# Top-k attention: eight candidates of the smaller halves instead of sixteen, a guarded second computation, and a mask by ReLU and GpSimd

## The chip, the cores and the metric

The kernel runs on one core of a Trainium2 chip. The metric is device time in microseconds of one execution, lower is better. The core has five engines that run side by side and meet only at semaphores: TensorE (PE in the profile, with its weight loads as PEld), VectorE (DVE), ScalarE (ACT), GpSimd (POOL) and SyncE (SP), which here issues nearly all transfers. Each engine takes its instructions strictly in the order in which the program lists them.

## The reference, cut to what matters

The inputs are q, k and v of shape (8, 8, 576, 64) (batch, heads, sequence, head width), a gain of 512 and two weight matrices of 512 x 2048 and 2048 x 512.

```python
# attention, per batch and head
scores = scale * q @ k.T                          # 576 x 576, scale = 1/8
kth = 32nd largest score of each row
scores = where(scores >= kth, scores, -1e9)
attn = exp(scores - row_max); attn /= attn.sum + 1e-9
x = attn @ v                                      # heads side by side: (8, 576, 512)
# feed-forward
xn = (x - mean) / sqrt(var + 1e-6) * g_ln
out = x + relu(xn @ w_ch1) @ w_ch2
```

All is fp32. There are 8 x 8 x 576 = 36,864 rows of 576 scores, and the 32nd largest of each has to be found.

## The kernel before, in words

**Units.** The attention is cut into 160 units. A full unit (128 of them) is 128 query rows of two heads of one batch: two tiles `t` of 128 x 576 scores. A rest unit (32) holds the last 64 rows of the sequence for two heads, as one tile of 128 x 576. A job is a batch and a pair of heads (`hp`) with its groups of units; units of a group share one transposed probability tile `pt`.

**One unit, step by step.** `scores` (L412 matmuls, L393 copies by ACT) writes the scores to `sc`. `halve` (L433 and on) splits each row into two halves of 288 and keeps, for each pair of columns, the larger in `hi` and the smaller in `lo`: the larger by a DVE maximum (L433), the smaller by two exact integer passes on POOL (a - hi, L438, and + b, L441); only the first unit takes a DVE minimum (L436). `select` then finds the 32 largest. DVE's MAX8 gives the eight largest of a row, and a match-replace (a load of the eight values, then a pass) overwrites them with -3e38. First two MAX8 over `lo` (L453), with a replace between (L448), put the 16 largest of the smaller halves into the last 16 columns of `hi`, which is therefore 304 wide; then four rounds of MAX8 over `hi` (L462), with replaces between the rounds (L448), give the 32 largest, eight at a time. The first eight hold the row's maximum (`u.top`), the last of the fourth eight is the threshold (`u.thr`). `prepare` makes the exponential's bias from both (L478 on DVE for the first units, L483 and L484 on POOL later). `mask` (L489) is one ACT operation, a leaky ReLU of (threshold - score) with slope 2^-90, so that scores at or over the threshold keep a scaled value and the others stay large; `weigh` (L499) is the exponential, with the row sums as its second output. The probabilities are transposed, either by PE (`turn`: L553, L573, L574, L582, with ACT copies into `pt`) or, for units marked `moved`, by DVE in blocks and through DRAM (`move`: L531, two DMAs L536 and L539). `values` (L607, L614) multiplies by v, `place` (L626, L649) normalises into rows of x.

**Feed-forward.** When two row tiles of x are complete they form a `Block` (18 in all): statistics on DVE (L677, L678), centring on POOL (L686), transposes (L711), hidden products (L752, ReLU on ACT L775), projections (L909, in seven products instead of eight, with POOL sums L839 to L845 and joins L889, L893), scaling (L730) and the residual (L723). The first block projects plainly (L791). Weights arrive in pieces that ACT, POOL and DVE convert (L190 to L208) until about unit 17 (`CONVERTING`).

**Order.** The order is written out by hand: the program disables the scheduler, and the order of issue in the source is the order on each engine. The main loop has one step `n` per unit. Step n selects unit n, masks unit n - 1 (`mk`), weighs and transposes unit n - 2 (`ex`), and computes the scores of unit n + 2; in the first units (`EARLY`, the first eight) mask and weigh of unit n - 1 stand together near the step's start. Between these pieces `fill()` inserts feed-forward matmuls from the list `todo`. How many is decided by a planner: during the conversion of weights from the difference of assumed DVE and PE costs of a step (`dve_cost`, with DVE_UNIT = 8.6 and DVE_REST = 5.0), later by spreading evenly what is left up to the next block. Buffers that matter here: `sc` five, `hi` two, `lo` one, `e` (masked scores and probabilities) two, five PSUM banks for scores and transposes and three for products.

## Time and profile before

| | |
|---|---|
| Time, median of 3 runs | 1653.51 us (1651.67 to 1654.98) |
| Profiled execution, own time | 1652.03 us |
| Its span, first to last instruction | 1650.0 us |
| Mean granted TensorE clock | 0.959 |
| Selection over `hi`: MAX8 L462 | x1152, mean 462 ns |
| Selection over `hi`: replace L448 | x864, mean 460 ns |
| Selection over `lo`: MAX8 L453 | x576, mean 443 ns |
| Selection over `lo`: replace L448 | x288, mean 443 ns |
| Larger halves, DVE L433 | x160, mean 692 ns |
| Smaller halves, POOL L438 and L441 | x159 each, mean 1286 and 1285 ns |
| Mask and exponential, ACT L489 and L499 | x288 each, mean 782 and 783 ns |

A line of the profile names the source line, the engine, the operation, output and input with shapes, the count, then the engine's busy time in us and the mean of one in ns; behind the last bar stands the time in which the engine was idle just before these instructions, and what ended it. A window row gives the stretch in us, its length, busy time and count for each engine, then the granted TensorE clock, the share of the DMA engines and GB/s. A timeline row gives start, length, engine, line and operation. Durations of neighbouring instructions on one engine can overlap.

### The profile page before, as it was taken

The page shows a single profiled execution, that of the slowest core. Times are in us where ns is not written, and L with a number is a line of the kernel's source. Part 1 is how long each engine was busy: PE and PEld are TensorE (multiplying, and loading weights), DVE is VectorE, ACT ScalarE, POOL GpSimd, SP SyncE. Part 2 cuts the span into 40 slices and gives each one's busy share as a digit, 9 for nine tenths or more (in the row PEclk, how much of TensorE's full clock was granted, in tenths as well). Part 3 has the DMA queues.
Part 4 walks back from the last instruction along what each step waited for, and adds up shares of the span by engine and source line. Part 5 has one row for each costly group of instructions (what it writes and reads, how often), then busy time and mean ns, then how long its engine had stood idle before and what let it go on. Part 6 is the DMA issues. An engine that isn't in the chain of part 4 may idle for free.

```text
span 1650.0 us, 27871 instructions
## 1 busy us (share of the span) xinstructions
PE 1504.6 (91%) x7897; PEld 1134.6 (69%) x7897; DVE 1458.2 (88%) x4652; ACT 1064.0 (64%) x2712; POOL 958.4 (58%) x1492
## 2 busy tenths in 40 slices
PE   3569998999888988999999998999989999999998
PEld 1336566767655766777677776777767777778887
DVE  5999898999999999999999999999999999994000
ACT  6987876767655756667566665676657766654411
POOL 4778759555555564656564656474646564655243
PEclk6679999999999999999999999999999999999999
DMA  7533355113454455535555456535564455532211
GB/s 200 131 128 114 100 119 143 55 58 90 124 156 136 124 144 160 159 94 139 171 165 162 114 128 177 168 105 135 153 184 134 130 131 169 154 114 83 73 51 51
DMA packets 358945, 211.46 MB, mean 128 GB/s; under 512 B 250756, under 2 KB 331144, under 8 KB 358792
## 3 DMA queue, kind: packets, MB, share of 16 engines
q1 hardware_dynamic: 354056, 209.10, 44.9%
q10 hardware_dynamic: 4736, 0.59, 0.3%
q8 instruction: 63, 1.03, 0.3%
q14 instruction: 90, 0.74, 0.2%
HBM read 145.62 MB, written 63.96 MB: 127 GB/s over the span
## 4 chain that ended last, share of the span: by engine, by line
DVE 65%; PE 19%; POOL 7%; ACT 3%; DMA 2%; issue 2%; SPq 1%; DVEq 0%; POOLq 0%; ACTq 0%
DVE m L462 19%; DVE hi L448 17%; DVE hi L453 10%; PE hps L752 8%; PE ops L909 6%; DVE lo L448 6%; DVE hi L433 5%; DVE sc L531 4%; PE av L607 2%; PE scps L412 1%; POOL lo L441 1%; POOL lo L438 1%; DVE st L677 1%; DVE kT L342 1%; POOL w L208 1%
## 5 line engine op out<-in xcount | busy, mean ns | idle before, releaser
L752 PE MATMUL hps<-xT,w 128*128 128x256 f32 x2304 | 547.5, 383 | 1.9 <-ACT xT L714 1.9
L462 DVE MAX8 m<-hi 128x8 f32<-128x304 f32 x1152 | 489.5, 462 | 3.3
L752 PEld LDWEIGHTS hps<-xT,w 128*128 128x128 f32 x2304 | 422.0, 191 | 71.6 <-issue 15.4
L438 POOL TENSOR_TENSOR lo<-sc,hi 128x576 int32<-128x576 int32 (+1 forms) x159 | 204.5, 1286 | 451.3 <-DVE hi L433 224.3
L448 DVE MATCH_REPLACE8 hi<-m,hi 128x304 f32<-128x304 f32 x864 | 391.1, 460 | 0.0
L909 PE MATMUL ops<-w,h 128*128 128x256 f32 x1360 | 325.6, 383 | 1.7 <-POOL h L845 1.7
L909 PEld LDWEIGHTS ops<-w,h 128*128 128x128 f32 x1360 | 248.6, 191 | 42.9 <-issue 6.9
L453 DVE MAX8 hi<-lo 128x8 f32<-128x288 f32 x576 | 234.2, 443 | 7.5 <-POOL lo L441 6.4
L393 ACT COPY sc<-scps 128x288 f32<-128x288 f32 x576 | 195.8, 409 | 58.2 <-PE scps L412 21.0
L499 ACT ACTIVATE e<-e,bias 128x576 f32<-128x576 f32 x288 | 225.5, 783 | 9.6 <-POOL bias L484 9.0
L489 ACT ACTIVATE e<-sc,m 128x576 f32<-128x576 f32 x288 | 225.0, 782 | 5.8 <-DVE m L462 3.2
L441 POOL TENSOR_TENSOR lo<-lo,sc 128x576 int32<-128x576 int32 (+1 forms) x159 | 204.3, 1285 | 12.5
L607 PE MATMUL av<-pt,vb 128*64 128x256 f32 (+2 forms) x1088 | 158.1, 435 | 47.2 <-DMA pt<-turned 24.5
L607 PEld LDWEIGHTS av<-pt,vb 128*64 128x64 f32 x1088 | 81.6, 149 | 115.4 <-issue 42.2
L775 ACT ACTIVATE h<-hps 128x512 f32<-128x512 f32 x144 | 86.1, 598 | 115.8 <-PE hps L752 115.3
L412 PE MATMUL scps<-kT,late_qT 64*128 64x288 f32 (+3 forms) x832 | 128.7, 411 | 7.9 <-ACT pt L565 5.3
L909 PE MATMUL ops<-wt,s 128*128 128x256 f32 x544 | 129.2, 381 | 0.0
L448 DVE MATCH_REPLACE8 lo<-hi,lo 128x288 f32<-128x288 f32 x288 | 125.6, 443 | 0.0
L531 DVE STREAM_TRANSPOSE sc<-e 128x512 f32<-128x512 f32 x144 | 93.8, 685 | 35.0 <-ACT e L499 34.9
L433 DVE TENSOR_TENSOR hi<-sc 128x576 f32<-128x576 f32 (+1 forms) x160 | 110.8, 692 | 10.0 <-ACT sc L393 10.0
L553 PE MATMUL tp<-ident,e 128*128 128x128 f32 x576 | 91.7, 284 | 29.9 <-ACT e L499 28.3
L412 PE MATMUL scps<-kT,qT 64*128 64x288 f32 x512 | 92.3, 461 | 27.9 <-DVE qT L342 26.1
(96 smaller groups left out, 1843.9 us busy)
## 6 DMA issues: line engine op xcount, KB each, us to landing
turned<-sc SPq DMA_DIRECT2D x72, 512.0 KB, 2.6
pt<-turned SPq DMA_DIRECT2D x288, 128.0 KB, 2.9
w<-forms SPq DMA_DIRECT2D x136, 256.0 KB, 3.8
vb<-in_v_dram SPq DMA_DIRECT2D x136, 128.0 KB, 3.2
raw<-in_moe_w_ch_dram SPq DMA_DIRECT2D x32, 512.0 KB, 4.2
kT<-kept SPq DMA_DIRECT2D x36, 288.0 KB, 3.3
kin<-in_k_dram SPq DMA_DIRECT2D x128, 72.0 KB, 2.5
kept<-kT SPq DMA_DIRECT2D x32, 288.0 KB, 3.1
```

The lines of the kernel that those rows point to most:

```text
L393: nc.scalar.copy(u.sc[:, t, s * HALF : (s + 1) * HALF], made[s][t][:, 0:HALF])
L412: nc.tensor.matmul(ps[i * R : i * R + ql, o : o + width], qT[r, q0 : q0 + ql], kT[r, k0 : k0 + width], start=True, stop=True,)
L438: nc.gpsimd.tensor_tensor(lo.bitcast(I32), a.bitcast(I32), hi.bitcast(I32), ALU.subtract)
L441: nc.gpsimd.tensor_tensor(lo.bitcast(I32), lo.bitcast(I32), b.bitcast(I32), ALU.add)
L448: nc.vector.match_replace(x[:, t], m[:, t, :], x[:, t], LOWEST)
L453: nc.vector.max(u.hi[:, t, o : o + 8], u.lo[:, t])
L462: nc.vector.max(m[:, t, :], u.hi[:, t])
L489: nc.scalar.activation(u.e[:, t], u.sc[:, t], AF.Prelu, bias=u.thr[:, t, 7:8], scale=-1.0, alpha=SLOPE)
L499: nc.scalar.activation(u.e[:, t], u.e[:, t], AF.Exp, bias=u.bias[:, t : t + 1], scale=-scale / SLOPE, accum_out=g.den[:, col : col + 1],)
L607: nc.tensor.matmul(av[h * D : (h + 1) * D, 0 : g.nq], vb[:, h * J + c, :], g.blocks[:, h, 0 : g.nq // 32, c, :], start=(c == 0), stop=False,)
L752: nc.tensor.matmul(ps[0][:, side * N : (side + 1) * N], w1[:, c, f * P : (f + 1) * P], self.xT[:, c, 0:N], start=(c == 0), stop=(c == NC - 1),
L909: nc.tensor.matmul(bank[name][:, 0:Q], a(j), rhs, start=first and j == 0, stop=(j == G - 1), skip_group_check=not first,)
```

## The change

- `select` takes only the eight largest of the smaller halves (`low_rounds=1`): one MAX8 over `lo` per tile, no replace. `hi` is 296 wide instead of 304; its first two rounds read only the 288 larger halves, and the eight candidates of `lo` are found in the second round and join in the third and fourth.
- `halve` takes the smaller halves by a DVE minimum for every unit; POOL's two integer passes are gone.
- `mask` becomes a ReLU of 2^90 x (threshold - score) on ACT, followed by a POOL subtraction of the scores; the exponential's scale and bias follow. `prepare` writes the scaled threshold (`edge`) and the bias into spare columns of the threshold's tile: two small operations, on DVE for the first units and on POOL later.
- `watch` notes, per unit, the eighth candidate of the smaller halves minus the threshold; a value of zero or more means that a ninth could have belonged to the 32. DVE reduces these notes every 16 units, and `tell` turns them into one flag at the end.
- The kernel becomes `compute(low_rounds=1)`, then a read of the flag on every engine, and behind a branch the whole `compute(low_rounds=2)` again.
- The planner's DVE_UNIT becomes 6.0 + 1.65 x low_rounds = 7.65 and DVE_REST 0.58 of it. In the first units both masks are issued before both exponentials. Two small statistics tiles come from a pool with two buffers instead of four.

```diff
         u.lo = lopool.tile([P, 2, HALF], FP32, tag="lo", name="lo")
-        u.hi = hipool.tile([P, 2, HALF + TOP_K // 2], FP32, tag="hi", name="hi")
+        u.hi = hipool.tile([P, 2, HALF + 8 * low_rounds], FP32, tag="hi", name="hi")
         a, b = u.sc[:, 0:nt, 0:HALF], u.sc[:, 0:nt, HALF:S]
         lo, hi = u.lo[:, 0:nt], u.hi[:, 0:nt, 0:HALF]
         nc.vector.tensor_tensor(hi, a, b, ALU.max)
-        if u.i == 0:
-
-            nc.vector.tensor_tensor(lo, a, b, ALU.min)
-            return
-        nc.gpsimd.tensor_tensor(
-            lo.bitcast(I32), a.bitcast(I32), hi.bitcast(I32), ALU.subtract
-        )
-        nc.gpsimd.tensor_tensor(lo.bitcast(I32), lo.bitcast(I32), b.bitcast(I32), ALU.add)
+        nc.vector.tensor_tensor(lo, a, b, ALU.min)
...
-        if i == 0:
-            for o in range(HALF, HALF + TOP_K // 2, 8):
+        if i == 1:
+            for r in range(low_rounds):
+                o = HALF + 8 * r
                 for t in nt:
                     nc.vector.max(u.hi[:, t, o : o + 8], u.lo[:, t])
-                if o == HALF:
+                if r < low_rounds - 1:
                     for t in nt:
-                        replace(u.hi[:, :, o : o + 8], t, u.lo)
-            return
-        for r in ((0,), (1,), (2, 3))[i - 1]:
-            pl = brief_small if r in (1, 2) else small
-            m = pl.tile([P, 2, 8], FP32, tag=f"m{r}", name=f"m{r}")
+                        replace(u.hi[:, :, o : o + 8], t, u.lo[:, t])
+        width = HALF + 8 * low_rounds if i > 1 else HALF
+        pl = brief_small if i in (1, 2) else small
+        m = pl.tile([P, 2, 8], FP32, tag=f"m{i}", name=f"m{i}")
+        for t in nt:
+            nc.vector.max(m[:, t, :], u.hi[:, t, 0:width])
+        if i < TOP_K // 8 - 1:
             for t in nt:
-                nc.vector.max(m[:, t, :], u.hi[:, t])
-            if r < TOP_K // 8 - 1:
-                for t in nt:
-                    replace(m, t, u.hi)
...
     def prepare(u):
...
+        u.bias, u.edge = u.thr[:, 0:nt, 5], u.thr[:, 0:nt, 6]
+        if doubt is not None:
+            watch(u)
+        eng = nc.vector if u.i < CONVERTING else nc.gpsimd
+        eng.tensor_scalar(u.edge, u.thr[:, 0:nt, 7], STEEP, 0.0, ALU.mult, ALU.add)
+        eng.tensor_scalar(u.bias, u.top[:, 0:nt, 0], -scale, 0.0, ALU.mult, ALU.add)
+
+    def watch(u):
...
+        eng.tensor_tensor(
+            watched[:, c : c + nt], u.hi[:, 0:nt, HALF + 7], u.thr[:, 0:nt, 7], ALU.subtract
+        )
+        if u.i % 16 == 15 or u.i == N - 1:
+            u.ends_watch = True
+
+    def settle_watch():
+
+        for out, first, op in ((0, 0, ALU.max), (33, 1, ALU.min)):
+            nc.vector.tensor_reduce(
+                watched[:, out : out + 1], watched[:, first : first + 33],
+                mybir.AxisListType.X, op,
+            )
+
+    def tell():
+
+        w = hpool.tile([P, J * P], FP32, tag="h", name="tell")
+        nc.gpsimd.memset(w[:], 0.0)
+        nc.vector.tensor_scalar(w[:, 1:2], watched[:, 33:34], -1.0e38, None, ALU.is_le)
+        nc.vector.tensor_scalar(w[:, 0:1], watched[:, 0:1], 0.0, None, ALU.is_ge)
+        nc.vector.tensor_tensor(w[:, 0:1], w[:, 0:1], w[:, 1:2], ALU.max)
+        ps = brief("tell")
+        nc.tensor.transpose(ps[:, 0:P], w[:, 0:P], ident[:])
+        nc.vector.tensor_reduce(w[0:1, P : P + 1], ps[0:1, 0:P], mybir.AxisListType.X, ALU.max)
+        nc.vector.tensor_copy(doubt, w[0:1, P : P + 1])
 
     def mask(u, t):
         if u.e is None:
             u.e = epool.tile([P, 2, S], FP32, tag="e", name="e")
         nc.scalar.activation(
-            u.e[:, t], u.sc[:, t], AF.Prelu, bias=u.thr[:, t, 7:8], scale=-1.0, alpha=SLOPE
+            u.e[:, t], u.sc[:, t], AF.Relu, bias=u.edge[:, t : t + 1], scale=-STEEP
         )
+        nc.gpsimd.tensor_tensor(u.e[:, t], u.e[:, t], u.sc[:, t], ALU.subtract)
...
-            u.e[:, t], u.e[:, t], AF.Exp, bias=u.bias[:, t : t + 1], scale=-scale / SLOPE,
+            u.e[:, t], u.e[:, t], AF.Exp, bias=u.bias[:, t : t + 1], scale=-scale,
...
-    DVE_UNIT, DVE_REST, DVE_MOVE, DVE_TURN = 8.6, 5.0, 1.4, 1.45
+    DVE_UNIT = 6.0 + 1.65 * low_rounds
+    DVE_REST, DVE_MOVE, DVE_TURN = 0.58 * DVE_UNIT, 1.4, 1.45
...
         if early:
             for t in range(2):
                 mask(ex, t)
+            for t in range(2):
                 weigh(ex, t)
...
+        if doubt is not None and at(n - 1) and at(n - 1).ends_watch:
+            settle_watch()
+            if n == N:
+                tell()
...
+    doubt = ctx.enter_context(tc.tile_pool(name="doubt", bufs=1)).tile(
+        [1, 1], I32, tag="doubt", name="doubt"
+    )
+    compute(tc, *operands, low_rounds=1, doubt=doubt[:])
+    again = nc.values_load(
+        doubt[:], min_val=0, max_val=1,
+        skip_runtime_bounds_check_because="a comparison's result",
+    )
+    with tc.If(again > 0):
+        compute(tc, *operands, low_rounds=2, doubt=None)
```

## The prediction

> **What bounds the kernel now.** I read the busy shares first, then the chain that ended last, then the windows by stage, because the chain changes engine on the way.
>
> ```profile
> PE 1504.6 (91%) x7897; PEld 1134.6 (69%) x7897; DVE 1458.2 (88%) x4652; ACT 1064.0 (64%) x2712; POOL 958.4 (58%) x1492
> ...
> DVE m L462 19%; DVE hi L448 17%; DVE hi L453 10%; PE hps L752 8%; PE ops L909 6%; DVE lo L448 6%; DVE hi L433 5%; DVE sc L531 4%; PE av L607 2%; PE scps L412 1%; POOL lo L441 1%; POOL lo L438 1%; DVE st L677 1%; DVE kT L342 1%; POOL w L208 1%
> ```
>
> Two engines are near full by busy time, and the chain (65% DVE, 19% PE) runs on the selection of the 32 largest. Three middle stages, with 0 to 200 before them and a last stretch after 1500 (columns: PE, weight load, DVE, ACT, POOL busy, then clock and DMA):
>
> ```profile
> 0.00:50.00 50.00, 15.17 (x53) 9.41 (x55) 31.94 (x95) 34.37 (x69) 28.25 (x34) 0.65 0.66 165
> 50.00:200.00 150.00, 117.65 (x531) 74.61 (x532) 140.51 (x472) 129.15 (x296) 115.64 (x103) 0.84 0.44 130
> ...
> 200.00:400.00 200.00, 189.93 (x1092) 136.46 (x1091) 191.19 (x618) 145.65 (x387) 131.50 (x196) 0.99 0.34 87
> 400.00:700.00 300.00, 267.39 (x1397) 198.38 (x1395) 295.05 (x933) 189.57 (x506) 160.62 (x270) 0.95 0.51 142
> 700.00:1500.00 800.00, 771.36 (x4129) 592.79 (x4128) 786.76 (x2500) 521.48 (x1359) 458.45 (x767) 0.99 0.50 142
> ```
>
> From 400 to 1500 DVE is 98% busy: it sets the pace. From 1500 on it has nothing to do; PE runs the last projections alone for 150 us. So a saving on DVE counts until PE is full, and the question is how near PE is.
>
> **PE's room: a rule against a row.** By busy time PE has 96% in 700 to 1500, so 29 us of room in 800. The Trainium skill (Trainium Kernel Development and Optimization, Performance Expectations) says that matmul busy time is a poor measure of how near TensorE is to its limit, because matmuls are pipelined, and that the weight loads are a better one. The trace lets me count instead, from spacings in the last stretch, where PE never waits:
>
> ```profile
> 1505.28 1.95 PE L607 MATMUL av<-pt,vb 128*64 128x256 f32 x16
> 1507.16 0.70 PE L614 MATMUL av<-pt,ends 128*128 128x256 f32 x2
> ...
> 1591.14 27.79 PE L752 MATMUL hps<-xT,w 128*128 128x256 f32 x128
> 1618.77 10.52 PE L909 MATMUL ops<-w,h 128*128 128x256 f32 x48
> ```
>
> Start to start that is 27.63/128 = 0.216 us for one of L752 or L909, 1.88/16 = 0.118 for L607, 0.53/2 = 0.265 for L614; likewise 0.146 for L412 (8 in 1.17), 0.11 for a transpose, and 0.432 for L791 (twice the columns of L752, an estimate). Times the counts of each line in a stage:
> - 200 to 400: 399 of L752 and L909 (86.2), 36 of L791 (15.6), 192 of L607 (22.6), 24 of L614 (6.4), 214 of L412 (31.2), 227 transposes (25): 187 us of need in 200.
> - 400 to 700: 737, 0, 192, 24, 278, 166: 247 in 300.
> - 700 to 1500: 2341, 0, 544, 68, 706, 470: 742 in 800.
>
> The need is 93%, 82% and 93%; the rule is right that busy time hides room. Mixed work has reached at most 97% (96.7 us of need between 1100 and 1200, counted the same way), so I divide by 0.97: 193, 255 and 765 us. By busy time the last stage could give at most 29 us, by the count 35, and the middle one 33 or 45.
>
> **Part 1: DVE, selection.** One full unit (two heads by 128 rows), from the timeline:
>
> ```profile
> 902.39 0.07 DVE L448 MATCH_VALUE_LOAD lo<-hi,lo 128x8 f32 x1
> 902.45 0.44 DVE L448 MATCH_REPLACE8 lo<-hi,lo 128x288 f32<-128x288 f32 x1
> ...
> 903.24 0.81 DVE L453 MAX8 hi<-lo 128x8 f32<-128x288 f32 x2
> 903.96 0.84 DVE L462 MAX8 m<-hi 128x8 f32<-128x304 f32 x2
> ...
> 905.59 0.75 DVE L433 TENSOR_TENSOR hi<-sc 128x576 f32<-128x576 f32 x1
> 906.26 0.85 DVE L462 MAX8 m<-hi 128x8 f32<-128x304 f32 x2
> ```
>
> - Removed: the pair of replaces on the smaller halves (902.39 to 903.24, 0.85 us) and the second pair of maxima (903.24 to 903.96, 0.72 us): 1.57 us. I use starts, not durations: durations overlap, and their sum would be a fifth more.
> - Narrowed: rounds 0 and 1 read 288 columns instead of 304 (8 instructions), rounds 2 and 3 read 296 (6). The rows give (0.460 - 0.443)/16 = 1.06 ns a column, so 8 x 16 + 6 x 8 = 176 columns, 0.19 us.
> - Added: the minimum of the halves, now always on DVE, two inputs, 128x576. It has one row of its own (L436, 752 ns, at 12 us); its twin L433 takes 0.67 from start to start.
>
> Net 1.57 + 0.19 - 0.67 = 1.09 us for each of 128 full units, half for each of 32 rest units: 157 us. Back go the watch's reductions (10 sets of two), the larger preparation of the first units (one more small operation, 0.2 us, in some 17) and the verdict's five small ones: about 9 us, at rows of 0.16 to 0.20. Net 148 of 1458, 9.9 us per 100.
>
> **Part 2: POOL.** It loses the two integer passes (409 us) and the bias pair (56), and gains the subtraction e - sc, 288 of 128x576 at 1.41 (the median of L438 for that size; fp32 at 128x512 takes 1.27 in L723, the same per column): 406; and three small operations for 143 units: 86. It ends near 985. The GPSIMD Engine Reference (section 1, Specifications) speaks against the new minimum: POOL shares its SBUF interfaces with DVE and contends with DVE operations of two SBUF inputs. Row: L433 is 749 ns median with POOL running, L436 752 at 12 us, before POOL's first integer pass at 24, so DVE pays nothing. By the rule POOL could be held for all of the new minimum, 144 x 0.67 = 96 us, and reach 1080, still under 70%. I take 0 and keep 96 for POOL; it doesn't set the end.
>
> **Part 3: the new wait.** ACT's mask (L489, now a ReLU of the same 782 ns) also waits for POOL's edge, and ACT's exponential (L499) for POOL's subtraction, where it waited only for the bias. Behind L499 on ACT queue the four copies of the next scores (L393), the ReLU of the hidden products (L775) and the evacuations; PE waits for their banks. Between the second mask and its exponential lie the first exponential (0.97 with its readout) and four copies (1.49): 2.5 us against a subtraction of 1.41. So 1.1 us of POOL queue is covered. What exceeds it are the eight L845 in a row (3.7 us), the runs of L839 to L841 (1.4) and L723 (1.27): some 2.6 us x 17 blocks = 44 us of ACT waiting at most, and ACT is idle 443 us of these 1300. If a fifth reaches PE: 8 us; ends 0 and 44. Also POOL must read `hi` before DVE reuses its buffer two units on, half a step of cover; when PE paces, DVE can wait freely.
> In the first eight units mask and exponential follow each other directly: ACT waits 1.41 - 0.78 = 0.63 us for the first subtraction and 2.82 - 1.41 - 0.97 = 0.44 for the second, 9 us in all, double with one weight pass (L206, 1.27) ahead in POOL's queue, while ACT has 129 of 150. DVE, at 140 of 150, gains up to 10 there. I take 0, ends -10 and +18.
>
> **Part 4: order of the filling and the end.** The planner's DVE cost per unit drops from 8.6 to 7.65, so until the weights are converted it puts 0.95 us less projection into each of about 10 steps: 9.5 us of PE work move behind 200. Stage 400 to 700 has room for part; I take +5 (0 to 10). At the end every engine reads a flag and branches over the second computation. No row shows such a read; the nearest is the closing wait, 1.3 us. DMA: Bandwidth & Descriptors (Latency and other measured facts) puts a floor of 0.6 us on such a load, and Runtime: NRT & Kernel Launch (Instruction fetch mechanics) says that a branch far off must first fetch its target. I take +4 (1 to 10). The branch itself isn't taken: a row needs 8 pairs with both members among its 32 largest, and counting the reference's 36,864 rows the most is 6.
>
> **Sum.** Stage by stage, after = the larger of DVE's time less its saving and PE's need/0.97:
> - 200 to 400: max(200 - 20, 193) = 193, gain 7.
> - 400 to 700: max(300 - 30, 255) = 270, gain 30.
> - 700 to 1500: max(800 - 79, 765) = 765, gain 35.
> - 0 to 200: 0. From 1500: the same matmuls, 0.
>
> 72 - 8 - 5 - 4 = 55. The profiled execution took 1652.0 (span 1650.0): 1597. The median of the runs is 1653.5, 1.5 above: **1599 us**, 3.3% faster.
>
> **Rivals.**
> - *DVE's whole saving arrives.* If PE can run at its full spacing, or early stages shorten too, the gain is 30 + 13 + 58 + 10 - 9 (Parts 3 and 4 small) = 102: 1552, with half of that excess 1575. For it: need is only 93%. Against: no mixed 100 us exceeded 97%.
> - *The change moves nothing.* DVE's work was hidden by a chain through ACT and POOL: 1640 to 1655. Against: DVE's idle time is 2% between 400 and 1500, and its waits are for few things.
> - *Slower: ACT's exponential waits for POOL.* Place: L499 behind the subtraction. Price: every us of wait that ACT can't absorb stops copies and so PE. ACT idles 443 us over about 140 units, 3.2 us a unit; the gain is worth 0.4. If all the idle time can be used, it decides at 3.6 us of wait per unit; if a third, at 1.5. At 2 us a unit and a third usable, 140 x (2.0 - 1.06) = 132 lost, 1599 + 132 = 1731; a milder 1.5 gives 1661. For it: POOL's queue holds bursts of 3.7 us. Against: they come once per block, not per unit.
> - *The second computation runs:* about 3200.
>
> **How the numbers follow.** Chances: PE becomes the bound, 0.60 (its own range 1580 to 1620); more of the saving, 0.20; nothing moves, 0.08; POOL's wait, 0.11; branch taken, 0.01. A measurement here tells 0.2% (3 us) from no change. Faster: 0.60 + 0.20 + 0.06 of the third + 0 = 0.86; same 0.02; slower 0.12. The range takes the first three cases: 1565 to 1650.
>
> **What would show it.** Right: about 148 us less DVE busy, MAX8 on the smaller halves x288, no replace on them; PE need near 97% from 200 on; DVE idle time in 200 to 1500 rising to some 8%, ended by ACT's copies of scores; PE's last stretch still some 150 us long; POOL near 985. Wrong: the exponential's idle time, now 9.6 us, in the hundreds and ended by POOL; PE idle ended by ACT; instructions of the second computation in the trace; a stretch after the last output of more than 10 us.

## The result, and the profile after

The changed kernel takes 1655.8 us (median of 12 runs, 1649.3 to 1658.7) where the kernel before, on the same chips, takes 1652.2 (12 runs). The ratio is 1.0015 with a 95% interval of 1.0004 to 1.0026. So there is no gain; if anything it is slower by some 0.15%, inside the 0.2% that I had named as hard to tell from no change. The forecast was 1599. The second computation did not run: the trace holds 27,426 instructions, fewer than the 27,871 of before.

From the page of the changed kernel, the busy times and the groups that answer to those of before (busy time and mean ns of one; then idle time of the engine ahead of them, and what ended it):

```profile
PE 1508.0 (91%) x7898; PEld 1132.7 (68%) x7898; DVE 1334.3 (81%) x3990; ACT 1067.4 (65%) x2712; POOL 1078.1 (65%) x1607
...
POOL o L882 0%; POOL o L716 0%; POOLq L1330 0%; ACT t L876 0%
...
L484 POOL TENSOR_TENSOR e<-e,sc 128x576 f32<-128x576 f32 x288 | 412.4, 1435 | 419.4 <-ACT e L481 403.1
...
L429 DVE MAX8 m<-hi 128x8 f32<-128x296 f32 (+1 forms) x1152 | 464.3, 444 | 1.1
...
L492 ACT ACTIVATE e<-e,m 128x576 f32<-128x576 f32 x288 | 224.8, 780 | 52.8 <-POOL e L484 52.4
...
L407 DVE TENSOR_TENSOR hi<-sc 128x576 f32<-128x576 f32 (+1 forms) x160 | 120.1, 751 | 157.4 <-POOL watched L452 135.7
```

DVE did get its saving: 1334 us of work where it had 1458. It no longer sets the pace by its work, and yet the end did not move. The chain of this run (second piece of the fence) breaks off after a few instructions at the closing branch, so it cannot be compared with the chain of before. The last group says where the saved time went: ahead of the maximum of the halves, L407, DVE now stands idle for 157 us, and 136 of them end with POOL's watch, L452. In the kernel before the same instruction waited 10 us in all. The wait of the changed kernel (total in us, times, longest), and the group of the kernel before:

```profile
DVE hi L407 <- POOL watched L452: 135.7, 57, 11.4
```

```profile
L433 DVE TENSOR_TENSOR hi<-sc 128x576 f32<-128x576 f32 (+1 forms) x160 | 110.8, 692 | 10.0 <-ACT sc L393 10.0
```

By stage (columns as in the prediction):

```profile
0.00:50.00 50.00, 15.05 (x48) 8.87 (x49) 33.93 (x85) 31.26 (x64) 25.99 (x33) 1.00 0.62 165
50.00:200.00 150.00, 102.97 (x448) 64.95 (x447) 127.35 (x373) 118.33 (x266) 108.68 (x89) 0.78 0.39 116
200.00:400.00 200.00, 188.29 (x1054) 130.08 (x1053) 170.87 (x521) 146.53 (x382) 144.91 (x197) 0.98 0.33 87
400.00:700.00 300.00, 274.76 (x1455) 203.56 (x1454) 270.66 (x812) 196.25 (x516) 189.88 (x306) 0.95 0.50 141
700.00:1500.00 800.00, 783.06 (x4193) 601.54 (x4192) 716.02 (x2153) 530.53 (x1388) 534.57 (x850) 0.99 0.49 145
```

Two things are to be seen. Between 50 and 200 PE does 448 matmuls where it did 531, and every engine does less: the kernel starts worse. Between 400 and 1500 DVE has 113 us of idle time where it had 18, but PE's busy time rises by only 19. Counted with the spacings of the prediction, PE's need in 700 to 1500 is 755 of 800, where a kernel in which PE sets the pace needs 776 at the 97% that I had assumed.

To place the loss in time I compare when the maximum of the halves starts for the same unit in both kernels (us from the start of the span, from the timelines):

| unit | before | after | difference |
|---|---|---|---|
| 4 | 59.3 | 58.8 | -0.5 |
| 8 | 99.1 | 110.0 | +10.9 |
| 12 | 143.1 | 161.8 | +18.7 |
| 24 | 254.6 | 274.9 | +20.3 |
| 64 | 611.5 | 623.2 | +11.7 |
| 152 | 1422.9 | 1426.5 | +3.6 |
| end of span | 1650.0 | 1653.6 | +3.6 |

Twenty microseconds are lost by unit 24, nearly all of them between units 4 and 12; seventeen are won from unit 24 to 152, where I had forecast 72, and the end is as long as before. So there are two questions: what is lost early, and what eats the gain in the middle.

### The profile page after: what moved, and what is told of

Read it like the earlier page. It is cut to its first block, busy times and chain, and to the rows that moved or that the text cites. A ratio compares the mean times of both kernels' runs of the same rounds, so it can differ in the third digit from the quotient of the medians.

```text
span 1653.6 us, 27426 instructions
## 1 busy us (share of the span) xinstructions
PE 1508.0 (91%) x7898; PEld 1132.7 (68%) x7898; DVE 1334.3 (81%) x3990; ACT 1067.4 (65%) x2712; POOL 1078.1 (65%) x1607
## 5 line engine op out<-in xcount | busy, mean ns | idle before, releaser
L484 POOL TENSOR_TENSOR e<-e,sc 128x576 f32<-128x576 f32 x288 | 412.4, 1435 | 419.4 <-ACT e L481 403.1
L429 DVE MAX8 m<-hi 128x8 f32<-128x296 f32 (+1 forms) x1152 | 464.3, 444 | 1.1
L415 DVE MATCH_REPLACE8 hi<-m,hi 128x288 f32<-128x288 f32 (+1 forms) x864 | 378.2, 444 | 0.0
L492 ACT ACTIVATE e<-e,m 128x576 f32<-128x576 f32 x288 | 224.8, 780 | 52.8 <-POOL e L484 52.4
L407 DVE TENSOR_TENSOR hi<-sc 128x576 f32<-128x576 f32 (+1 forms) x160 | 120.1, 751 | 157.4 <-POOL watched L452 135.7
L408 DVE TENSOR_TENSOR lo<-sc 128x576 f32<-128x576 f32 (+1 forms) x160 | 120.9, 756 | 0.0
L546 PEld LDWEIGHTS tp<-ident,e 128*128 128x128 f32 x576 | 73.9, 148 | 65.7 <-ACT e L492 51.6
L421 DVE MAX8 hi<-lo 128x8 f32<-128x288 f32 x288 | 118.0, 446 | 0.0
L386 PEld LDWEIGHTS scps<-kT,late_qT 64*128 64x128 f32 (+1 forms) x832 | 72.0, 168 | 59.4 <-issue 23.5
```

What stands on the lines that cost most here:

```text
L386: nc.tensor.matmul(ps[i * R : i * R + ql, o : o + width], qT[r, q0 : q0 + ql], kT[r, k0 : k0 + width], start=True, stop=True,)
L408: nc.vector.tensor_tensor(lo, a, b, ALU.min)
L415: nc.vector.match_replace(x, m[:, t, :], x, LOWEST)
L429: nc.vector.max(m[:, t, :], u.hi[:, t, 0:width])
L484: nc.gpsimd.tensor_tensor(u.e[:, t], u.e[:, t], u.sc[:, t], ALU.subtract)
L492: nc.scalar.activation(u.e[:, t], u.e[:, t], AF.Exp, bias=u.bias[:, t : t + 1], scale=-scale, accum_out=g.den[:, col : col + 1],)
```

## The experiments

**Selection alone: is the bound right?** The kernel before with eight candidates only, nothing else of the change; POOL's integer passes stay, and there is no guard. Its mask is a ReLU without the leak, of the same size and on the same engine.

```diff
-        u.hi = hipool.tile([P, 2, HALF + TOP_K // 2], FP32, tag="hi", name="hi")
+        u.hi = hipool.tile([P, 2, HALF + 8], FP32, tag="hi", name="hi")
...
-            for o in range(HALF, HALF + TOP_K // 2, 8):
+            for o in range(HALF, HALF + 8, 8):
...
-                if o == HALF:
-                    for t in nt:
-                        replace(u.hi[:, :, o : o + 8], t, u.lo)
...
-            u.e[:, t], u.sc[:, t], AF.Prelu, bias=u.thr[:, t, 7:8], scale=-1.0, alpha=SLOPE
+            u.e[:, t], u.sc[:, t], AF.Relu, bias=u.thr[:, t, 7:8], scale=-1.0
```

> The kernel before with eight candidates of the smaller halves instead of sixteen and nothing else: smaller halves by the two integer passes on POOL, no subtraction on POOL, no watch, no branch. Its mask is a plain ReLU of (threshold - score) in the place of the leaky one, so every kept score weighs the same; the operation has the same size and engine. DVE's work falls by some 220 us (1.57 + 0.1 us per full unit). Theory A (PE is full in the middle once DVE gives way, and the rest of the changed kernel's loss is its first 150 us): no early loss, the middle gains what PE allows, 15 to 30 us, so 1622 to 1638 us against 1652 before. Theory B (the new wait through POOL sets the middle's pace): without it the saving arrives, 1580 to 1605 us.

Measured: 1580.0 us, ratio 0.956 (0.953 to 0.959), at the low end of theory B's range. Its busy times, and then its stage from 700 to 1400:

```profile
PE 1489.4 (94%) x7897; PEld 1127.1 (71%) x7897; DVE 1222.3 (77%) x3788; ACT 1066.9 (68%) x2712; POOL 970.4 (61%) x1492
```

```profile
700.00:1400.00 700.00, 696.29 (x3783) 534.55 (x3781) 603.12 (x1857) 482.10 (x1255) 432.24 (x716) 1.00 0.54 152
```

Here PE is the bound: busy 99.5% of the stage, with a counted need of 678 in 700, which is 97%. From unit 24 to 152 the kernel gains 70 us against the one before. That is near the 72 of my sum, but partly by chance: DVE saves more here, some 220 us, and with that PE would pace 400 to 700 too, and the same sum gives 7 + 44 + 35 = 86. The ceiling of 97% holds from 700 on (counted need 777 of 800); from 400 to 700 this kernel reaches 92% (275 of 300). So PE has room of about the forecast size, and the changed kernel does not reach it. The rest of the change costs 76 us on top of this kernel.

**Mask alone.** The changed kernel with sixteen candidates again, without the guard, with the old planner costs: minimum on DVE, ReLU, POOL's subtraction.

```diff
-    DVE_UNIT = 6.0 + 1.65 * low_rounds
-    DVE_REST, DVE_MOVE, DVE_TURN = 0.58 * DVE_UNIT, 1.4, 1.45
+    DVE_UNIT, DVE_REST, DVE_MOVE, DVE_TURN = 8.6, 5.0, 1.4, 1.45
...
-    compute(tc, *operands, low_rounds=1, doubt=doubt[:])
...
+    compute(tc, *operands, low_rounds=2, doubt=None)
```

> The other half alone: sixteen candidates as before, but the smaller halves by the DVE minimum, the mask by ReLU and POOL's subtraction, no watch, no branch, the planner's costs as before. DVE has some 90 us more than before, POOL about the same own work. Theory A: DVE paces again, and the early loss of some 18 us comes on top: 1652 + 18 + (60 to 90) = 1730 to 1760 us. Theory B: each wait for POOL is added, 1780 us or more.

Measured: 1764.4 us, ratio 1.069 (1.066 to 1.071), just above the range of theory A, with DVE busy 1583 us. The mask's half of the change costs 112 us here, where DVE has no saving to pay for it; 21 of them are lost by unit 24, which starts at 275.7. The rest goes with DVE's busy time, 125 us more than before; what the minimum alone costs is not separated. The two halves of the change are one trade: the selection frees DVE, the mask fills it again.

**No guard, and the guard without its watch.** The first leaves out the whole guard (watch, verdict, read, branch, second computation). The second keeps everything but the watch of each unit.

```diff
-    compute(tc, *operands, low_rounds=1, doubt=doubt[:])
...
-    with tc.If(again > 0):
-        compute(tc, *operands, low_rounds=2, doubt=None)
+    compute(tc, *operands, low_rounds=1, doubt=None)
```

> The changed kernel without its guard: no watch, no reductions, no flag, no branch, no second computation. DVE no longer has to wait for POOL's watch before it reuses the buffer of the larger halves (136 us of DVE idle time in the changed kernel). Theory A: that idle time is slack of an engine that does not pace; only the end's read and branch go: 1649 to 1655 us. Theory B: the wait is the pace, and 1595 to 1625 us follow.

```diff
         u.bias, u.edge = u.thr[:, 0:nt, 5], u.thr[:, 0:nt, 6]
-        if doubt is not None:
-            watch(u)
+        if u.i % 16 == 15 or u.i == N - 1:
+            u.ends_watch = True
```

> The changed kernel without the watch of each unit: reductions, flag, read by every engine, branch and second computation stay, so the flag says nothing. It prices the end. By the estimate on record the read and branch cost 1 to 10 us: 1628 to 1637 us (1627 without any guard). If reading the flag or the doubled program costs more, 1640 us or above.

Measured: 1627.4 us (ratio 0.984, 0.982 to 0.986) and 1625.5 us (0.984, 0.982 to 0.986). The guard costs 28 us, and all of that comes with one small operation per unit, on POOL from unit 17 on (minimum, median and maximum duration in ns, in the changed kernel):

```profile
L452 POOL TENSOR_TENSOR watched<-hi,m x143: 179/196/208, 228.3 to 1536.9; 128x2 f32<-128x2 f32 x112, 128x1 f32<-128x1 f32 x31
```

The verdict, the flag read by all engines, the branch and the doubled program cost nothing that can be measured. The first of these runs was between its two forecasts, which had asked whether the guard costs next to nothing or most of what is missing. Without the guard, units 24 to 152 gain 38 us against the kernel before; with it 17, with the selection alone 70.

**No subtraction in the first 17 units.** POOL's subtraction is left out there, with a plain ReLU for the mask and the bias made as in the kernel before; the rest is the changed kernel, guard included. A second kernel does the same without the guard.

```diff
+        if u.i < CONVERTING:
+            nc.scalar.activation(
+                u.e[:, t], u.sc[:, t], AF.Relu, bias=u.thr[:, t, 7:8], scale=-1.0
+            )
+            return
         nc.scalar.activation(
             u.e[:, t], u.sc[:, t], AF.Relu, bias=u.edge[:, t : t + 1], scale=-STEEP
         )
...
```

> The changed kernel, but the 17 units during which weights are converted take the mask without POOL's subtraction (a plain ReLU of threshold - score straight into the exponential; in these units every kept score weighs the same). Theory A: the 18 us that units 4 to 12 lost come back and stay: 1634 to 1640 us. Theory B: the early units reach 200 us sooner but the middle's pace is POOL's, so part is lost again: 1643 to 1656 us.

> Without the guard, and the first 17 units without POOL's subtraction (in these units every kept score weighs the same). The two gave 28 and 30 us alone. If they are separate losses, as the places of the units say (units 4 to 12, and units 24 to 152), they add up: 1594 to 1603 us. If one hides the other, 1612 to 1624 us.

Measured: 1625.4 us (0.985, 0.982 to 0.987), better than both forecasts, and 1599.3 us (0.968, 0.966 to 0.971). The subtraction of the first units costs 30 us with the guard in place and 28 without it, so the two losses add up. Unit 24 starts at 240.3 in the first of them, against 274.9 in the changed kernel and 254.6 before. How the loss comes about stands in the changed kernel's timelines of one early unit, ACT's first (start, duration, engine, line; in brackets the idle time ahead and what ended it):

```profile
57.32 1.44 ACT L481 ACTIVATE e<-sc,m 128x576 f32<-128x576 f32 x2
61.54 0.78 ACT L492 ACTIVATE e<-e,m 128x576 f32<-128x576 f32 x1 [2.78 <-POOL e L484]
...
62.91 0.77 ACT L492 ACTIVATE e<-e,m 128x576 f32<-128x576 f32 x1 [0.50 <-POOL e L484]
```

and POOL's:

```profile
58.18 4.69 POOL L484 TENSOR_TENSOR e<-e,sc 128x576 f32<-128x576 f32 x2 [3.97 <-ACT e L481]
```

and DVE's, at the same time:

```profile
58.16 0.74 DVE L174 TENSOR_SCALAR size<-size 128x512 uint32<-128x512 uint32 x2
58.83 0.74 DVE L407 TENSOR_TENSOR hi<-sc 128x576 f32<-128x576 f32 x1
59.50 0.74 DVE L408 TENSOR_TENSOR lo<-sc 128x576 f32<-128x576 f32 x1
60.17 0.16 DVE L1233 RECIPROCAL den<-den 128x4 f32<-128x4 f32 x1
```

The mask is ready at 58.2, the first exponential starts at 61.5, and ACT does nothing for 2.8 us between. I had forecast 0.6 for that wait, from a subtraction of 1.41. But DVE's L174, L407 and L408 fill 58.16 to 60.2: if POOL can do nothing in these 2.0 us, its subtraction ends at 58.2 + 2.0 + 1.4 = 61.6, which is when ACT goes on. The next experiment bears on this.

**Do POOL and DVE exclude each other?** A stretch in the middle of the changed kernel, from 523.8 to 525.3 (all engines; these four lines of it):

```profile
523.74 0.19 POOL L444 TENSOR_SCALAR m<-m 128x1 f32<-128x1 f32 x1
...
523.87 0.75 DVE L407 TENSOR_TENSOR hi<-sc 128x576 f32<-128x576 f32 x1
524.01 1.33 POOL L445 TENSOR_SCALAR m<-m 128x1 f32<-128x1 f32 x1
...
524.54 0.75 DVE L408 TENSOR_TENSOR lo<-sc 128x576 f32<-128x576 f32 x1
```

L444 and L445 do the same kind of work on one column. L444 takes 0.19 us. L445 begins while DVE runs the maximum and takes 1.33: it ends at 525.3, when the minimum ends. To test this, a kernel without the guard computes the two halves by a reduction over pairs, which has one input from SBUF, the on-chip memory that holds these tiles, instead of two, and gives the same result:

```diff
-        nc.vector.tensor_tensor(hi, a, b, ALU.max)
-        nc.vector.tensor_tensor(lo, a, b, ALU.min)
+        pairs = u.sc[:, 0:nt].rearrange("p t (h n) -> p t n h", h=2)
+        nc.vector.tensor_reduce(hi, pairs, mybir.AxisListType.X, ALU.max)
+        nc.vector.tensor_reduce(lo, pairs, mybir.AxisListType.X, ALU.min)
```

> Without the guard (1627 us), the larger and the smaller halves are taken by DVE reductions over pairs of columns, one input each, instead of tensor-tensor operations of two inputs. Each goes over 1152 values per full unit instead of writing 576, so DVE has about 1 us more per full unit. Theory C: with no DVE operation of two inputs in the steps, POOL's operations take their undisturbed times again (subtraction 1.41, sums 0.46, small ones 0.19 to 0.20) and POOL's busy time falls from 1043 us to 950 to 970; the reductions' longest is near their median. The time is then DVE's: 1630 to 1700 us. Theory D (POOL's times grew for another reason): POOL stays at 1030 us or more.

Measured: 1669.2 us (1.011, 1.009 to 1.013). It is slower than its counterpart of 1627.4, because the two reductions cost DVE 399 us where maximum and minimum cost 274. The question it answers is POOL's. The small operation of the changed kernel (minimum, median and maximum duration in ns), and then the same line of this one:

```profile
L445 POOL TENSOR_SCALAR m<-m x143: 191/195/1534, 228.9 to 1537.4; 128x2 f32<-128x2 f32 x112, 128x1 f32<-128x1 f32 x31
```

```profile
L446 POOL TENSOR_SCALAR m<-m x143: 191/193/195, 220.8 to 1553.8; 128x2 f32<-128x2 f32 x112, 128x1 f32<-128x1 f32 x31
```

Every one of 143 now takes 0.19 us, though DVE is busier (1473 us) than in any of the other kernels but the mask-only one. POOL's busy time is 953 us where the counterpart had 1043, for the same instructions. So the maxima, the replaces and one-input reductions of DVE leave POOL alone, and the two-input maximum and minimum stop it. The early wait shows the same. At the same place in this kernel DVE again runs L174 twice and then the two halves, now as reductions, and POOL's pair of subtractions is

```profile
58.91 3.29 POOL L485 TENSOR_TENSOR e<-e,sc 128x576 f32<-128x576 f32 x2 [3.96 <-ACT e L482]
```

instead of 4.69 us; ACT's first exponential waits 1.37 us instead of 2.78. So 1.4 us of the changed kernel's wait are the maximum and the minimum. Of the rest, 0.5 us go with L174, a DVE operation of one SBUF input that collides too: an undisturbed pair takes 2.77 us (at 71.58 in the same run), and in the changed kernel L174 itself lasted from 0.41 to 1.63 us. The text at the start says that engines meet only at semaphores; these two also meet in this way. The holding goes the other way too: without the guard, the two-input maximum takes longer, as its group in the counterpart's page and then its durations (ns) show:

```profile
L407 DVE TENSOR_TENSOR hi<-sc 128x576 f32<-128x576 f32 (+1 forms) x160 | 148.7, 929 | 40.9 <-ACT sc L367 40.4
```

```profile
L407 DVE TENSOR_TENSOR hi<-sc x160: 436/750/1954, 11.5 to 1467.2; 128x576 f32<-128x576 f32 x128, 128x288 f32<-128x288 f32 x32
```

Its longest, at 36.8, is 1.95 us: its own 0.75 and 1.2 of a subtraction that was already running (from 36.5 on).

**Four other places for the watch.** If the 28 us are the wait for the buffer `hi`, then a watch that doesn't make DVE wait for POOL should give them back. First, the watch on DVE, straight after the last maxima of the unit; with it, in a second kernel, also the early subtraction on DVE:

```diff
-        if doubt is not None:
-            watch(u)
...
-        eng = nc.vector if u.i < CONVERTING else nc.gpsimd
-        eng.tensor_tensor(
+        nc.vector.tensor_tensor(
             watched[:, c : c + nt], u.hi[:, 0:nt, HALF + 7], u.thr[:, 0:nt, 7], ALU.subtract
...
             select(u, 3)
+            if doubt is not None:
+                watch(u)
```

> The changed kernel with its whole guard, but the watch is one small DVE operation right after the fourth round of the selection instead of one on POOL a step later. The run without the guard took 1627 us and the changed kernel 1656, and units 24 to 152 went 21 us faster without it. Theory B1 (DVE waits to reuse the buffer of the larger halves until POOL, whose queue stands behind ACT's mask, has read it): 1628 to 1638 us, and DVE's idle time ended by the watch, 136 us, is gone. Theory B2 (it is the guard's other parts: the reductions, the flag, the branch): 1648 us or more.

> The watch on DVE, and in the 17 units during which weights are converted the subtraction of the scores on DVE instead of POOL; the whole computation and its guard. If the early loss (about 20 us, units 4 to 12) and the buffer's wait (about 21 us between units 24 and 152) are separate, they add up: 1603 to 1617 us, faster than both kernels. If they share a cause, 1622 to 1632 us.

Measured: 1649.0 us (0.999, 0.997 to 1.000) and 1656.0 us (1.003, 1.002 to 1.004). Both miss: the first lies in the range of B2, whose reason the kernel without the watch rules out, and the second is above both ranges. The wait for the buffer is gone, but the watch is itself an operation of two SBUF inputs (durations in ns, of the first kernel):

```profile
L449 DVE TENSOR_TENSOR watched<-hi,m x160: 159/165/1391, 28.0 to 1512.2; 128x2 f32<-128x2 f32 x128, 128x1 f32<-128x1 f32 x32
```

Two columns wide, 0.165 us in the median, and up to 1.39, as long as one of POOL's subtractions: one wait was swapped for another. DVE's busy time is 58 us above that of the kernel without the guard. Moving the early subtraction to DVE as well gives that engine more work and more operations that collide: unit 24 starts at 284.1, later than in the changed kernel.

Next, DVE copies the candidate to a spare column, from which POOL makes its watch:

```diff
+                nc.vector.tensor_copy(u.thr[:, 0:n8, 4], u.hi[:, 0:n8, HALF + 7])
...
-            watched[:, c : c + nt], u.hi[:, 0:nt, HALF + 7], u.thr[:, 0:nt, 7], ALU.subtract
+            watched[:, c : c + nt], u.thr[:, 0:nt, 4], u.thr[:, 0:nt, 7], ALU.subtract
```

> The changed kernel with its whole guard, and the watch still on POOL, but DVE first copies the eighth candidate (two values a row) out of the buffer of the larger halves, so that POOL reads the copy and DVE alone frees the buffer. It tells the buffer's wait from POOL's own time. B1: as with the watch on DVE, 1628 to 1640 us. B3 (the watch costs by its 0.2 us and its place in POOL's queue, 143 x 0.2 = 29 us of POOL): no change, 1650 to 1656 us.

Measured: 1644.6 us (0.994, 0.993 to 0.996), between the two forecasts. Some 11 of the 28 us are back. The copy collides too (durations in ns):

```profile
L1291 DVE COPY m<-hi x160: 153/170/1335, 28.2 to 1510.5; 128x2 f32<-128x2 f32 x128, 128x1 f32<-128x1 f32 x32
```

Then ACT makes the copies, and DVE compares them every eight units:

```diff
+        nc.scalar.copy(seen[:, 0, c - 1 : c - 1 + nt], u.hi[:, 0:nt, HALF + 7])
+        nc.scalar.copy(seen[:, 1, c - 1 : c - 1 + nt], u.thr[:, 0:nt, 7])
```

> The changed kernel with its whole guard, but the watch leaves DVE and POOL alone: ACT copies the eighth candidate and the threshold (two small copies a unit) into a small tile, and DVE compares the columns of eight units at once. The trace of the run with the watch on DVE shows that operation at 165 ns in the median and up to 1391, as long as a POOL subtraction. Theory C (a DVE operation of two inputs or a copy, and a POOL operation, wait for each other's end; the watch pays that once per unit wherever DVE or POOL does it): 1626 to 1636 us. If the guard's 28 us have another cause, 1643 to 1656 us.

Measured: 1678.7 us (1.018, 1.015 to 1.021), outside both forecasts and slower than the changed kernel. From the waits of this run (total, times, longest):

```profile
DVE hi L410 <- ACT seen L454: 118.6, 55, 8.7
```

ACT's copies do not collide (0.22 us in the median, 0.30 at most), and the wait is the same in kind: DVE again stands until another engine, in its own queue, has read two columns of the buffer. I had expected ACT to be there in time. The kernel is 23 us slower than the changed one though this wait is a little shorter; ACT's busy time is 29 us more, but what makes the difference is not separated.

Last, DVE makes the copy with MAX8 over the eight candidates, an operation that doesn't collide, early in the unit, and POOL watches the copy:

```diff
+                u.seen = seenpool.tile([P, 2, 8], FP32, tag="seen", name="seen")
+                for t in nt:
+                    nc.vector.max(u.seen[:, t, :], u.hi[:, t, HALF : HALF + 8])
...
-            watched[:, c : c + nt], u.hi[:, 0:nt, HALF + 7], u.thr[:, 0:nt, 7], ALU.subtract
+            watched[:, c : c + nt], u.seen[:, 0:nt, 7], u.thr[:, 0:nt, 7], ALU.subtract
```

> The changed kernel with its whole guard. Right after the candidates of the smaller halves are found, DVE takes the MAX8 of those eight into a small tile of its own (three buffers), and POOL's watch reads that tile a step later. MAX8 has one input and kept its duration in every run, so it neither waits for POOL nor holds it, and DVE alone frees the buffer of the larger halves. Theory E (the guard's 28 us are DVE held either by the buffer until another engine has read it, or, in the copies and the watch on DVE, by a POOL operation in progress): both go, 1628 to 1638 us. Theory F (the three small POOL operations per unit, or the reductions, cost it): 1644 to 1656 us, as with the copy.

Measured: 1634.2 us (0.989, 0.987 to 0.991), as expected. Its durations (ns):

```profile
L429 DVE MAX8 seen<-hi x288: 140/169/172, 15.4 to 1496.1; 128x8 f32<-128x8 f32 x144
```

None of 288 takes longer than 0.172 us, and the wait for the buffer is no longer among the waits. 22 of the 28 us are back, although POOL is as busy as in the changed kernel (1073 against 1078 us), and DVE's maximum takes longer than there (891 against 751 ns in the mean). So most of the guard's price is the release of `hi` by POOL, not the guard's instructions or the collisions; the other 6 us are the copies or what they delay, which is not separated here.

**The planner.** The kernel without the guard, with the planner's costs of before.

```diff
-    DVE_UNIT = 6.0 + 1.65 * low_rounds
-    DVE_REST, DVE_MOVE, DVE_TURN = 0.58 * DVE_UNIT, 1.4, 1.45
+    DVE_UNIT, DVE_REST, DVE_MOVE, DVE_TURN = 8.6, 5.0, 1.4, 1.45
```

> Without the guard (1627 us), the planner's DVE costs as in the kernel before (8.6 and 5.0), so that the early steps take as much projection work as before. By the estimate on record the lower cost loses up to 10 us: 1617 to 1627 us. If the early steps are held by ACT and POOL anyway, 1625 to 1634 us.

Measured: 1629.2 us (0.987, 0.985 to 0.989), against 1627.4 with the new costs; the ranges of their runs overlap. The planner's costs don't matter here.

**A version that beats both.** The MAX8 copy, and in the first eight units both masks issued at the start of the step, before the copies of the scores, so that POOL subtracts while ACT copies.

```diff
+        if early:
+            for t in range(2):
+                mask(ex, t)
         for x in due(n):
...
             for t in range(2):
-                mask(ex, t)
-            for t in range(2):
                 weigh(ex, t)
```

> The run before this one, and in the first eight units the two masks are issued at the step's start, ahead of the copies of the next scores, so that POOL's subtraction runs beside ACT's copies instead of between mask and exponential. If the early loss (18 us by unit 10) is ACT standing still for POOL's subtraction, 8 to 14 us of it come back: 1616 to 1626 us, with the whole computation and its guard. If it is POOL's queue and its collisions with DVE, 0 to 4 us: 1628 to 1636 us.

Measured: 1623.0 us (0.983, 0.981 to 0.985), 11 less than the kernel with the MAX8 copy and within the forecast, with the whole computation and the guard. Its busy times:

```profile
PE 1499.7 (93%) x7898; PEld 1128.9 (70%) x7898; DVE 1396.7 (86%) x4278; ACT 1067.9 (66%) x2712; POOL 1070.3 (66%) x1607
```

DVE is busier here than in the changed kernel (1397 against 1334 us), and the kernel is 33 us shorter: less of its time is spent waiting. Unit 12 starts at 147.8 instead of 161.8.

## Why the prediction was wrong

**The sum.** The parts as the runs give them, from the best kernel up: 1580 with the selection alone; 1599 with the minimum on DVE and the subtraction from unit 17 on; 28 for the subtraction in the first 17 units (1627); 28 for the watch (1656). The first step, 19 us, was not isolated: the two-input maximum takes 915 ns in the mean in the kernel of 1599 and 722 in the kernel of 1580, which has no two-input minimum on DVE, so the collisions and the added minimum are the likely cause, argued and not shown. This 19 is itself a difference of two: against the kernel of 1580, the kernel of 1599 starts unit 24 earlier by 13 us (238.6 against 252.1) and takes 36 us more from unit 24 to 152 (1134 against 1098). So the kernel of 1599, with a gain of 52 us, comes near my sum of 55 by luck: 16 us of it lie before unit 24, where I had 0, and only 35 between units 24 and 152.

**The middle stages, 72: not reached.** The count of PE's need, and 97% of full spacing as its ceiling, were right for the last middle stage in the kernel with the selection alone, and were not reached from 400 to 700 (92%); that this kernel gained 70 is in part chance, as said there. Busy time would have said 96% before and left at most 29 us for the last middle stage alone. What failed is the maximum of two terms: DVE's time less its saving, or PE's need. It holds only while neither engine waits for a third. Of the some 55 us by which the changed kernel missed the 72, 21 are the watch's (17 gained with it, 38 without). The other 34 belong to the rest of the mask, the minimum and maximum on DVE and POOL's subtraction; which of them, no run here separates.

**Part 3 is the step that failed most, and the runs show it.** It said of the buffer `hi` that POOL reads it with "half a step of cover; when PE paces, DVE can wait freely". I had named the wait and then set its price to nothing. POOL's watch stands behind POOL's subtraction, which stands behind ACT's mask, and ACT's mask behind ACT's queue. When that is late, DVE cannot start the next maximum, and DVE's later results are what PE needs. 57 waits, 136 us, up to 11.4 us each; 28 us of them reached the end. The room to wait freely was DVE's saving itself, 124 us measured, and the idle time ahead of L407 rose by 147 (157.4 against 10.0): the waits alone are larger than the saving.

**Part 3, the early units.** I took 0, with ends of -10 and +18. Measured: 20 us late at unit 24, and 28 to 30 us at the end when the subtraction is taken out, because then unit 24 comes earlier than before (240.3 against 254.6). The shorter selection alone does not do that (252.1 in the kernel of 1580, which keeps POOL's integer passes); that POOL has less to do there is the likely reason, not tested. The mechanism was named, ACT idle between mask and exponential; the term was mis-sized, 0.6 us for the first of the two waits in a unit against 2.8 in the one shown, because I priced the subtraction at its undisturbed time.

**Part 2, the rule against the row.** The Trainium skill (GPSIMD Engine Reference, Specifications) speaks of contention between POOL and DVE operations of two SBUF inputs, or in a 2-port mode, which no run here singles out; I took 0 by the rows of before and kept 96 us as a bound. POOL measured 1078, where I had 985: 93 more. The rule was right and the row misled. That 93 is so near the bound is luck: the bound counted the minimum alone, and both halves hold POOL. Before, POOL's first integer pass needed the maximum that DVE was computing, so POOL waited for the colliding operation by the order of the data (its idle time of 224 us that ended with L433), and the two engines took turns:

```profile
L438 POOL TENSOR_TENSOR lo<-sc,hi 128x576 int32<-128x576 int32 (+1 forms) x159 | 204.5, 1286 | 451.3 <-DVE hi L433 224.3
```

In the changed kernel the data no longer keeps them apart, and the watch drives them together: it frees `hi`, DVE starts the maximum, and the two small POOL operations behind the watch, L444 and L445, mostly run into it. They take 121 us in all, against 55 in the kernel with reductions: 66 of the 93 us. I added "it doesn't set the end", by POOL's share of 70%. True of POOL's total, but POOL's longer queue is part of both waits above.

**Part 1.** DVE's busy time fell by 124 us, not 148. The maximum and the minimum together take 241 us, where the maximum alone took 111 before: 222 for two undisturbed ones. So some 19 of the missing 24 us are maxima and minima that took longer than undisturbed ones. My 96 for the minimum is a price from start to start and cannot be set beside these sums of durations.

**Part 4.** 5 us for the planner and 4 for the end; both measured as nothing (1629.2 against 1627.4, 1625.5 against 1627.4). The end of the span after unit 152 is 227.1 us long in both kernels.

**The rivals.** The time is nearest to "the change moves nothing" (1640 to 1655), a case that I gave 0.08, but not for its reason: DVE's work was not hidden before, its saving was spent. The slower rival, the exponential's wait for POOL, had the right pair of engines and the wrong place: L492 idles 53 us in all, near the 44 that I had as its end, and far from the hundreds that would have decided. The wait that decided was DVE's, through a buffer. Of the signs, DVE's idle time was to rise to some 8% of 200 to 1500, ended by ACT's copies of scores; it rose to 11% (1300 less 171, 271 and 716), ended by POOL's watch.

**Open.** The 34 us in the middle and the 19 us above. A third buffer for `hi`, and eight candidates under the old leaky mask with the whole computation, were not tried.

## What to carry to other kernels

When work moves to a slower engine, price every buffer that this engine now releases: follow its read back through its whole queue, because one 0.2 us operation behind a long subtraction cost 28 us here. A duration taken from a trace in which two engines take turns says nothing of the time when they don't; look at what ordered them before calling a contention rule refuted. Count an engine's need by instructions and spacings to find the room, and then look for the wait that stops it from being used.

## What the hardware showed

- DVE operations of two SBUF inputs and POOL's exclude each other for whole instructions here, in both directions: a POOL operation of 0.19 us lasted up to 1.53, a maximum of 0.75 up to 1.95. A two-column DVE copy, with one input, was held the same way (0.17 in the median, 1.34 at most). The size of the held operation did not matter, only what it met.
- MAX8, the match-replaces and one-input reductions on DVE did not hold POOL, and a MAX8 of eight columns made a small copy that was never held: 0.17 us at most in 288.
- Reading a flag on every engine and branching over a second whole computation cost nothing measurable: 1625.5 us with it and 1627.4 without.
- The granted clock between 50 and 200 us was 0.84 before and 0.78 after, and 0.86 in the last version. It is not separated here whether the lower clock adds to the early loss or only follows from PE's idle time.
